# A spectral filter and a squared-ReLU feed-forward layer on one core: PSUM in three phases, index tables on GpSimd, constants folded into tables, the drain in another order

## The chip, the core and the metric

The kernel runs on one core of a Trainium2 chip. A core has five engines, each with its own instruction queue: TensorE (PE in the profile) multiplies matrices into PSUM, VectorE (DVE), ScalarE (ACT) and GpSimd (POOL) do element-wise work, and SyncE (SP) issues the transfers here. PSUM has eight banks of 512 float32 columns[...]. The metric is device time in microseconds from the start to the end of one execution. The span in the profile is the part of it between the first and the last instruction.

## The reference

The input x is 2048 rows by 512 columns in bfloat16. Two residual branches follow each other:

```python
h  = x + A(layernorm(x))          # A: irfft2(rfft2(x) * (w_r + 1j*w_i)) over both axes
h2 = h + B(layernorm(h))          # B: relu(h @ w1 + b1)**2 @ w2 + b2, 512 -> 1792 -> 512
```

A is a two-dimensional real Fourier transform over all 2048 rows and 512 columns, a product with a complex filter of 2048 by 257, and the inverse. So each row of the result of A depends on every row of x, and B can start only when A has ended for some rows.

## The kernel before

The 2048 rows are 16 tiles (g = 0 to 15) of 128 rows. The transforms are written as matrix products with sine tables that the kernel computes: GpSimd makes integer index tables (idxE, idxG, idxD), an index product such as `fiG` or `fiE` is formed by a multiplication with the partition number, and ScalarE turns it into bfloat16 with `Sin`. KF, EF, EI, GF and GI are the tables. EI and KI are transposes of EF and KF, made by a transfer (L432).

The first stage takes the mean and variance of each row tile (VectorE with bn_stats, L392, or ScalarE with two accumulating passes, L383 and L386, for tiles 5, 7, 9 and 11). In five batches of tiles, VectorE adds epsilon (L397), GpSimd raises to the power -0.5 (L399, `rs1`), and VectorE scales KF by it (L403, `KR`). TensorE multiplies x with KR (L415, L417, tiles p1 of PSUM), and ScalarE or VectorE copy the result into `Bt` (L423). Every tile of Bt is needed before the next step.

The middle stage works on eight pairs of blocks, pr = 0 to 7. For each: TensorE multiplies Bt with GF (p2, L485), a copy gives U (L494), TensorE multiplies with EF (p3, L511 to L550), ScalarE copies to AB (L517, L557), VectorE forms X (L564, only where the sum is not done by TensorE), then the products with the filter W, mA and mB (L574), their combination Z (L582) and the fold M (L593, L595). TensorE multiplies M with EI (p4, L609 to L615) and a copy gives T2 (L624).

The drain takes tiles 0 and 1 ahead of the others: d5 multiplies T2 with GI (L651), the copies are EO (L657), yt multiplies these back with a transposed output and is copied to UT0 (L664, L670), the first operand of the up-projection. The same rows in the straight order (py, L771 to L776) give the squares (L633, L786), the standard deviation `sd0` and, through a small matmul `sr` (L801), a row `srow` that scales the bias (L863).

The feed-forward stage goes over five chunks of rows, (0,2), (2,5), (5,9), (9,13), (13,16): up-projection (L859, 14 blocks), ReLU on ScalarE (L872), square on VectorE (L878), down-projection (L887), output (L896, L898). Between its matmuls TensorE also finishes A for the later tiles (p5 at L709 to L712, p6 at L732 or L739), which VectorE and ScalarE evacuate.

The order of instructions on each engine is decided while the program is built, by the class `Plan`. A task has an engine (or a choice of two), a cost, a priority, what it reads and writes, and perhaps a buffer of a pool with a set number of buffers. `run` repeatedly takes the task that can start first by these costs; tasks within SLACK of each other go by priority. `pin` then keeps this order in the program. Costs of transfers are issue times on SP and a lag to landing:

```python
add("SP", 1.2, lambda i=i: sy.dma_start(W[i][:, 0:9, :], wv[i][:, 0:9, 1:L + 1]), writes=[("Wn", i)],
    prio=20 + i, at=1.0, lag=7.0)
add("SP", 0.8, lambda i=i: sy.dma_start(W[i][:, 9:16, :], wx[i][:]), reads=[("wx", i)], writes=[("Wr", i)],
    prio=22 + i, lag=5.0)
```

The filter arrives in two parts of 9 and 7 block rows (`Wn`, `Wr`), each for the real and the imaginary half. The tables are scaled by WSC = 2/(2048*512) through GI (L454), where the last partition gets half of it through `hsc`. All PSUM tiles up to the drain come from one pool of four two-bank tiles (`mm_tile`); the feed-forward stage has one-bank tiles: three `ph`, two `po`, three `pp`. `warm` puts small matmuls on zeros in front of a tile where the planner sees TensorE idle.

Of the kernel before, what the change touches and what calls it, by code (L numbers as in the profile page):

```python
# [33 lines left out]
class Plan:  # L34
# [3 lines left out]
    SLACK = 0.15  # L38
# [51 lines left out]
    def run(self):  # L90
# [7 lines left out]
        while any(left.values()):  # L98
            best = None
            for e, ts in left.items():  # L100
                pick = None
                for t in ts:
# [13 lines left out]
                    if pick is None or r < pick[0] - self.SLACK:  # L116
                        pick = (r, t)
                    if r <= self.free[e] + 1e-9:
                        break
                if pick and (best is None or pick[0] < best[0] or (pick[0] == best[0] and e == "DVE")):  # L120
                    best = (*pick, e)
# [25 lines left out]
def kernel(  # L147
# [70 lines left out]
    hsc = fwd.tile([P, 1], FP32, name="hsc")  # L218
# [19 lines left out]
    ps = tc.alloc_tile_pool(name="ps", bufs=4, space=bass.MemoryType.PSUM)  # L238
# [4 lines left out]
    plan = Plan({"mm": 4, "U": 3, "AB": 3, "X": 2, "mA": 2, "mB": 2, "Z": 2, "M": 2, "st": 4, "EO": 2,  # L243
                 "ph": 3, "po": 2, "pp": 3, "rl": 6, "act": 2, "od": 2, "q": 2, "R": 3, "u2": 2, "qb": 2, "UT": 2, "ot": 3})
# [6 lines left out]
    def mm_tile(key, dt=FP32):  # L251
        T[key] = ps.tile([P, 4096 // mybir.dt.size(dt)], dt, tag="mm", name="m_" + str(key[0]))
        warm(T[key])
        return T[key]
# [8 lines left out]
    def lo(fi):  # L263
        return fi.bitcast(I16)[:, ::2]
# [35 lines left out]
    def iota(dst, pattern, base, cm):  # L300
# [17 lines left out]
    pool(0.1, lambda: gp.memset(mhalf[:], -0.5), 1.1, writes=["mhalf"])  # L318
# [4 lines left out]
    pool(0.1, lambda: gp.memset(hsc[:], WSC), 1.5, writes=["hsc0"])  # L323
    pool(0.2, lambda: gp.affine_select(out=hsc[:], in_=hsc[:], compare_op=ALU.not_equal, fill=0.5 * WSC, base=-(P - 1),
                                       pattern=[[0, 1]], channel_multiplier=1), 1.6, reads=["hsc0"], writes=["hsc"])

    pool(0.1, lambda: gp.memset(mv1[:], 0.0), 1.7, writes=["mv1z"])
# [13 lines left out]
    for t in range(2):  # L341
        for r in range(2):
            dve(0.36, lambda t=t, r=r: ve.tensor_scalar(fiG[:, t, r, :], idxG[:], pF[:, 3 + t:4 + t],
                                                        float((QT, HT)[r]), ALU.mult, ALU.add),
                0.6, reads=["pF", "idxG"], writes=[("fiG", t)], shared=True)
# [5 lines left out]
    act(1.28, lambda: sc.activation(fiE[0][:], idxE[:], ACT.Identity, scale=cE[:]), 0.3, reads=["idxE", "cE"],  # L351
        writes=["fiE0"])
# [12 lines left out]
    def fill(key, n, prio, reads=(), at=0.0):  # L365
        def go():
            p = mm_tile(key)
            for _ in range(n):
                mm(p[:, 0:512], lhsT=fz[:, 0:P], rhs=fz[:], start=True, stop=True)
        add("PE", n * 0.216, go, reads=["fz", *reads], writes=[key], prio=prio, alloc=("mm", key), at=at)  # L370
# [4 lines left out]
    ON_ACT = (5, 7, 9, 11)  # L375
    SQ = 6
    BATCH = ((0, 4), (4, 8), (8, 12), (12, 14), (14, 16))
    RT = float(1.0 / np.sqrt(D))
    for bi, (a, b) in enumerate(BATCH):
# [22 lines left out]
        for g in range(a, b):  # L402
            dve(0.22, lambda g=g: ve.tensor_scalar(flat(KR[:, g]), flat(KF[:]), rs1[:, g:g + 1], None, ALU.mult), z - 5,  # L403
                reads=[("rs", bi), "KF"], writes=[("KR", g)], shared=True)
    for j in range(8):
        key = ("p1", j)
        for i in range(2):
            g = 2 * j + i

            def s1(g=g, i=i, key=key):  # L410
                pt = mm_tile(key) if i == 0 else T[key]
                pv = pt[:].rearrange("p (t e i c) -> p t e i c", t=2, e=2, i=2)
                for t in range(2):
                    o = pv[:, t, :, i, :]
                    mm(o, lhsT=xs[:, g, P * t:P * t + P], rhs=KR[:, g, 0].unsqueeze(1).to_broadcast([P, 2, P]),  # L415
                       start=True, stop=False)
                    mm(o, lhsT=xs[:, g, 256 + P * t:256 + P * t + P], rhs=KR[:, g], start=False, stop=True)  # L417
            add("PE", 0.46, s1, reads=[("KR", g), ("x", g)], order=[("p1a", j)] * i,
                writes=[key, ("p1a", j) if i == 0 else ("p1b", j)], prio=10 + 2 * j, alloc=("mm", key) if i == 0 else None)

        def e1(j=j, lo_=0, hi=2, eng=sc.copy):
            dst = Bt[:].rearrange("p e q (g s) -> p e g q s", s=8)[:, :, 2 * j + lo_:2 * j + hi]
            eng(dst, T["p1", j][:].rearrange("p (e i q s) -> p e i q s", e=4, i=2, q=16)[:, :, lo_:hi])  # L423
        if j < 5:
            act(0.93, e1, 10 + 2 * j, reads=[key], writes=["Bt"])
        else:
            for i in range(2):
                add(("ACT", "DVE"), (0.59, 0.67), lambda e, j=j, i=i, e1=e1: e1(j, i, i + 1, COPY[e]),
                    reads=[("p1a" if i == 0 else "p1b", j)], writes=["Bt"], uses=[key], prio=56 + 2 * j)
# [17 lines left out]
    for lt in range(4):  # L447
        pool(0.48, lambda lt=lt: gp.tensor_scalar(fiI[:, lt], idxD[:], pF[:, 5 + lt % 2:6 + lt % 2],
                                                  float((QT, HT)[lt // 2]), ALU.mult, ALU.add), 2.0,
             reads=["pF2", "idxD"], writes=["fiI"])  # L450
    act(1.07, lambda: sin_of(flat(GI[:]), lo(flat(fiI[:]))), 27.0, reads=["fiI", ("KR", 13)], writes=["GI0"])
# [482 lines left out]
```

## Time and profile before

| | us |
|---|---|
| median of 3 runs | 178.74 (178.45 to 178.90) |
| the profiled execution | 178.47 |
| its span | 176.7 |
| TensorE busy | 164.3 (93%) |
| VectorE busy | 125.7 (71%) |
| ScalarE busy | 112.0 (63%) |
| GpSimd busy | 11.8 (7%) |
| up-projection L859, 280 matmuls | 54.8 busy |
| down-projection L887, 224 matmuls | 51.8 busy |

The ends of matmuls are modelled and overlap, so TensorE's busy share is not its share of peak; starts are measured. The profile lists groups of instructions by line and shape, the chain of work that ended last, DMA issues with the time to landing, and timelines by engine, in which a row has its start, its length and, in brackets, the idle time before it with what ended it. Times in it count from the start of the span. The mean granted TensorE clock is 0.998 of full speed.

### The profile page before, as it was taken

What the parts mean: (1) busy time and instruction counts of PE and PEld (TensorE: products, weight loads), DVE (VectorE), ACT (ScalarE), POOL (GpSimd) and SP (SyncE); (2) the same over time, 40 slices, a digit from 0 to 9 for tenths busy, and PEclk for the clock granted to TensorE, in tenths of its full rate; (3) what the DMA queues carried; (4) which work ended last, traced back from release to release, by engine and by line L of the source; (5) the groups of instructions that cost most, each with busy time, mean ns of one, the idle gap of its engine ahead of it and who ended that gap; (6) DMA issues with size and microseconds to landing.
All of it is one profiled execution on the core that took longest, in us unless ns stands there. A gap on an engine that the chain in (4) does not pass through costs nothing.

```text
span 176.7 us, 3029 instructions
## 1 busy us (share of the span) xinstructions
PE 164.3 (93%) x1123; PEld 96.5 (55%) x1123; DVE 125.7 (71%) x358; ACT 112.0 (63%) x203; POOL 11.8 (7%) x32
## 2 busy tenths in 40 slices
PE   7989669999987799998999999999999999999991
PEld 4478546776664565556655454444554445455540
DVE  4999558989984497356998569989369896156331
ACT  8799729998673646657889268665358663066400
POOL 8844100000000000000000000000000000000000
PEclk9999999999999999999999999999999999999999
DMA  5959999970000000000000100001100000100010
GB/s 139 338 138 164 257 302 298 383 228 0 4 0 0 0 4 0 0 32 33 0 0 0 61 32 0 0 2 58 36 30 0 0 0 33 59 30 0 4 59 30
DMA packets 15600, 12.16 MB, mean 69 GB/s; under 512 B 6112, under 2 KB 14176, under 8 KB 15586
## 3 DMA queue, kind: packets, MB, share of 16 engines
q1 hardware_dynamic: 15586, 11.97, 23.9%
q8 instruction: 9, 0.15, 0.4%
q14 instruction: 5, 0.04, 0.1%
HBM read 8.92 MB, written 3.01 MB: 68 GB/s over the span
## 4 chain that ended last, share of the span: by engine, by line
PE 69%; DVE 12%; ACT 10%; issue 3%; DMA 3%; SPq 0%; DVEq 0%; ACTq 0%
PE ph L859 28%; PE po L887 28%; ACT Bt L423 3%; DMA xs<-in_A_x_dram 3%; DVE Z L582 2%; PE pp L837 2%; DVE mA L574 2%; DVE mB L574 2%; ACT junk L383 2%; PE m_p L485 2%; ACT junk L386 2%; PE pp L739 1%; PE ph L863 1%; DVE M L593 1%; ACT AB L557 1%
## 5 line engine op out<-in xcount | busy, mean ns | idle before, releaser
L859 PE MATMUL ph<-UT,W 128*128 128x384 bf16 (+2 forms) x280 | 54.8, 337 | 0.7 <-ACT UT L845 0.7
L887 PE MATMUL po<-W,act 128*128 128x512 bf16 x224 | 51.8, 379 | 0.0
L872 ACT ACTIVATE rl<-ph,b1f 128x384 bf16<-128x384 f32 (+1 forms) x56 | 34.9, 632 | 24.8 <-PE ph L859 22.5
L859 PEld LDWEIGHTS <-W 128*128 128x128 bf16 x280 | 26.0, 98 | 20.9 <-issue 0.8
L878 DVE TENSOR_TENSOR act<-rl 128x384 bf16<-128x384 bf16 (+2 forms) x70 | 25.4, 368 | 14.3 <-ACT rl L872 13.3
L887 PEld LDWEIGHTS <-act 128*128 128x128 bf16 x224 | 21.5, 98 | 24.3 <-issue 0.4
L898 DVE TENSOR_TENSOR ot<-po,hb 128x512 bf16<-128x512 f32 x14 | 9.7, 692 | 17.1 <-PE po L887 16.9
L633 ACT ACTIVATE junk<-hs,nm 128x512 bf16<-128x512 bf16 x14 | 10.0, 714 | 1.9 <-DVE hs L760 1.8
L494 ACT CAST U<-m_p 128x1024 bf16<-128x1024 f32 (+1 forms) x8 | 9.2, 1194 | 2.7 <-DVE mhl L462 2.6
L763 DVE TENSOR_TENSOR hb<-hs,b2b 128x512 f32<-128x512 bf16 x16 | 10.7, 684 | 0.0
L760 DVE TENSOR_TENSOR hs<-pp,xs 128x512 bf16<-128x512 f32 x14 | 9.5, 685 | 0.3 <-PE pp L732 0.2
L624 ACT CAST T<-m_p 128x1024 bf16<-128x1024 f32 (+2 forms) x9 | 8.1, 904 | 2.5 <-PE m_p L615 1.8
L415 PE MATMUL m_p<-KR,xs 128*128 128x256 bf16 x32 | 7.2, 272 | 2.3 <-DVE KR L403 2.3
L824 ACT ACTIVATE u<-hs,nr,rs 128x512 bf16<-128x512 bf16 x8 | 6.2, 806 | 4.6 <-DVE nr L816 4.6
L485 PE MATMUL m_p<-GF,Bt 128*128 128x256 bf16 x64 | 8.0, 273 | 0.8 <-DVE Bt L423 0.8
L872 ACT ACTIVATE rl<-ph 128x256 bf16<-128x256 f32 x14 | 5.1, 383 | 5.7 <-PE ph L863 5.7
L557 ACT CAST AB<-m_p 128x1024 bf16<-128x1024 f32 x7 | 7.3, 1041 | 2.2 <-PE m_p L545 2.2
L249 PEld LDWEIGHTS <-fz 128*128 128x128 bf16 x115 | 7.6, 103 | 1.9 <-DVE pI L333 1.2
L615 PE MATMUL m_p<-EI,M 128*128 128x256 bf16 x56 | 7.9, 274 | 0.7 <-DVE M L593 0.5
L755 DVE TENSOR_TENSOR R<-q 128x127 bf16<-128x127 f32 x36 | 8.4, 285 | 0.0
L392 DVE BATCH_NORM_STATS2 st<-xs 128x6 f32<-128x512 bf16 x12 | 7.9, 663 | 0.0
L417 PE MATMUL m_p<-KR,xs 128*128 128x256 bf16 x32 | 7.2, 273 | 0.0
(191 smaller groups left out, 238.1 us busy)
## 6 DMA issues: line engine op xcount, KB each, us to landing
W<-in_B_w_dram SPq DMA_DIRECT2D x2, 1792.0 KB, 10.9
out_dram<-ot SPq DMA_DIRECT2D x16, 128.0 KB, 1.8
xs<-in_A_x_dram SPq DMA_DIRECT2D x3, 512.0 KB, 5.6
W<-wx SPq DMA_DIRECT2D x2, 448.0 KB, 6.6
W<-in_A_w_r_dram SPq DMA_DIRECT2D x1, 576.0 KB, 5.2
W<-in_A_w_i_dram SPq DMA_DIRECT2D x1, 576.0 KB, 7.2
xs<-in_A_x_dram SPq DMA_DIRECT2D x2, 256.0 KB, 3.7
wx<-in_A_w_r_dram SPq DMA_DIRECT2D x1, 448.0 KB
```

The lines of the kernel that those rows point to most:

```text
L485: mm(puv[:, q, e, :], lhsT=Bt[:, 2 * t + 1 - e, 2 * pr + q, :], rhs=gfv[:, t, :, e, :], start=(t == 0), stop=(t == 1))
L494: eng(U[:].rearrange("p q (c e) -> p q e c", e=2)[:, a:b], puv[:, a:b])
L557: sc.copy(t[:].rearrange("p u r c -> p (u r c)"), T["p3", pr][:])
L633: sc.activation(junk[:], src, ACT.Square, bias=nm1[:, g:g + 1], accum_out=ss2[:, g:g + 1])
L755: ve.tensor_tensor(o, x, y, (ALU.add, ALU.subtract, ALU.subtract, ALU.add)[k])
L760: dve(0.66, lambda g=g: ve.tensor_tensor(hs[:, g, :], T["p6", g][:], xs[:, g, :], ALU.add), z, reads=[("p6", g)], writes=[("hs", g)])
L763: dve(0.62, lambda g=g: ve.tensor_tensor(hb[:, g, :], hs[:, g, :], b2b[:], ALU.add), late + 180 + g, reads=[("hs", g), ("FW", 3), ("ph", c ...
L859: mm(p[:, 0:P * n], lhsT=W1[:, d, bass.ts(f, P)], rhs=(T["UT", c] if c else UT0)[:, d, 0:P * n], start=(d == 0), stop=(d == ND - 1 and c > 0))
L872: sc.activation(r[:, 0:P * n], T["ph", c, f][:, 0:P * n], ACT.Relu, bias=b1f[:, f:f + 1] if c else 0.0, scale=1.0)
L878: ve.tensor_tensor(t[:, f, 0:P * n], r[:, 0:P * n], r[:, 0:P * n], ALU.mult)
L887: mm(p[:], lhsT=T["act", c][:, f, bass.ts(i, P)], rhs=W2[:, f, :], start=(f == 0), stop=(f == NF - 1))
L898: ve.tensor_tensor(o[:], T["po", g][:], hb[:, g, :], ALU.add)
```

## The change

Six things change together.

- *The planner.* SLACK goes from 0.15 to 0.08, and a task is now picked by priority among all within SLACK of the earliest. The whole order is planned anew.
- *PSUM.* The program is planned in three phases. Phase a (the first stage) has two two-bank tiles (`mm`) and four one-bank tiles (`sg`); tiles 10 to 15 of p1 are one-bank tiles. Phase b has three two-bank tiles and two one-bank tiles; p2 of pairs 0 and 1, p3 of pair 0, mr and yt are one-bank tiles. Phase c has one `ph`, two `po`, three `pp` and the two `sg` that stay; up-projections rotate over ph, sg, sg. In the columns of p1 the two tiles of a two-bank tile now have a bank each.
- *Index tables.* The four `fiG` go from VectorE and `fiE[0]` from ScalarE to GpSimd. `fiI` is made after the last `rs1`, and the Sin for GI in the middle stage.
- *Constants.* WSC is a second multiplier of KR. `hsc` and the scaling of GI go; the half for the last partition is now a half for the last column of W (L-1), in place, by four GpSimd instructions, two for the first 9 rows and two for the last 7.
- *Statistics.* ScalarE takes tiles 3, 5, 7 and 9. The square-root table is loaded after p4 of pair 5 in place of 6.
- *Drain.* The last T2 is copied in halves by PSUM bank. d5 has a one-bank tile per product, from the pools of phase c. py comes ahead of the up-projection, UT0 of tile 0 is for VectorE and of tile 1 for ScalarE. Some waits in the feed-forward stage become orders.

```diff
-    SLACK = 0.15
+    SLACK = 0.08
...
-                    if pick is None or r < pick[0] - self.SLACK:
-                        pick = (r, t)
+                    cand.append((r, t))
                     if r <= self.free[e] + 1e-9:
                         break
+                pick = None
+                if cand:
+                    first = min(r for r, _ in cand) + self.SLACK
+                    pick = next(c for c in cand if c[0] <= first)
...
-    plan = Plan({"mm": 4, "U": 3, "AB": 3, "X": 2, "mA": 2, "mB": 2, "Z": 2, "M": 2, "st": 4, "EO": 2,
-                 "ph": 3, "po": 2, "pp": 3, "rl": 6, "act": 2, "od": 2, "q": 2, "R": 3, "u2": 2, "qb": 2, "UT": 2, "ot": 3})
+    plan = Plan({"mm": 2, "sg": 4, "U": 3, "AB": 3, "X": 2, "mA": 2, "mB": 2, "Z": 2, "M": 2, "st": 4, "EO": 2,
+                 "ph": 1, "po": 2, "pp": 3, "rl": 6, "act": 2, "od": 2, "q": 2, "R": 3, "u2": 2, "qb": 2, "UT": 2, "ot": 3})
...
-    pool(0.1, lambda: gp.memset(hsc[:], WSC), 1.5, writes=["hsc0"])
-    pool(0.2, lambda: gp.affine_select(out=hsc[:], in_=hsc[:], compare_op=ALU.not_equal, fill=0.5 * WSC, base=-(P - 1),
-                                       pattern=[[0, 1]], channel_multiplier=1), 1.6, reads=["hsc0"], writes=["hsc"])
...
-            dve(0.36, lambda t=t, r=r: ve.tensor_scalar(fiG[:, t, r, :], idxG[:], pF[:, 3 + t:4 + t],
-                                                        float((QT, HT)[r]), ALU.mult, ALU.add),
-                0.6, reads=["pF", "idxG"], writes=[("fiG", t)], shared=True)
+            pool(0.46, lambda t=t, r=r: gp.tensor_scalar(fiG[:, t, r, :], idxG[:], pF[:, 3 + t:4 + t],
+                                                         float((QT, HT)[r]), ALU.mult, ALU.add),
+                 1.95, reads=["pF", "idxG"], writes=[("fiG", t)])
...
-    act(1.28, lambda: sc.activation(fiE[0][:], idxE[:], ACT.Identity, scale=cE[:]), 0.3, reads=["idxE", "cE"],
-        writes=["fiE0"])
+    pool(1.4, lambda: gp.tensor_scalar(fiE[0][:], idxE[:], cE[:], 0.0, ALU.mult, ALU.add), 0.95, reads=["idxE", "cE"],
+         writes=["fiE0"])
...
-            dve(0.22, lambda g=g: ve.tensor_scalar(flat(KR[:, g]), flat(KF[:]), rs1[:, g:g + 1], None, ALU.mult), z - 5,
+            dve(0.22, lambda g=g: ve.tensor_scalar(flat(KR[:, g]), flat(KF[:]), rs1[:, g:g + 1], WSC, ALU.mult, ALU.mult), z - 5,
...
-                                                  float((QT, HT)[lt // 2]), ALU.mult, ALU.add), 2.0,
-             reads=["pF2", "idxD"], writes=["fiI"])
-    act(1.07, lambda: sin_of(flat(GI[:]), lo(flat(fiI[:]))), 27.0, reads=["fiI", ("KR", 13)], writes=["GI0"])
...
-    for e in range(2):
-        dve(0.35, lambda e=e: ve.tensor_scalar(GI[:, e::2], GI[:, e::2], hsc[:] if e else WSC, None, ALU.mult), 180.0,
-            reads=["GI0", "hsc"], writes=["GI"], shared=True)
+                                                  float((QT, HT)[lt // 2]), ALU.mult, ALU.add), 400.0,
+             reads=["pF2", "idxD", ("rs", 4)], writes=["fiI"])
...
+        act(1.07, lambda: sin_of(flat(GI[:]), lo(flat(fiI[:]))), 125.0, reads=["fiI"], writes=["GI"])
...
+    for k, (a, b) in (("n", (0, 9)), ("r", (9, 16))):
+        for i in range(2):
+            pool(0.15, lambda i=i, a=a, b=b: gp.tensor_scalar(W[i][:, a:b, L - 1:L], W[i][:, a:b, L - 1:L], 0.5, None,
+                                                              ALU.mult), 300.0,
+                 reads=[("W" + k, i)], writes=[("Wh" + k, i)])
...
+            plan.run()
+            ps.release()
+            psg = ctx.enter_context(tc.tile_pool(name="psg", bufs=2, space=bass.MemoryType.PSUM))
+            ps = tc.alloc_tile_pool(name="psb", bufs=3, space=bass.MemoryType.PSUM)
...
-            act(0.32, lambda: et(7, 0, 2), z, reads=[("p4", 7)], writes=["T2a"])
...
+            for h in range(2):
+                add(("ACT", "DVE"), (0.25, 0.22), lambda e, h=h, et=et: et(COPY[e], 7, h, 2, 0, 2), prio=z, reads=[("p4", 7)],
+                    writes=["T2a", ("T2a", h)])
+                add(("ACT", "DVE"), (0.53, 0.6), lambda e, h=h, et=et: et(COPY[e], 7, h, 2, 2, 16), prio=z + 90,
+                    reads=[("p4", 7)], order=["T2a"], writes=["T2", ("T2r", h)])
...
-        add(("ACT", "DVE"), (0.58, 0.67), ute, reads=[("yt", g, 2)], writes=[("UT", 0)], uses=[("yt",)], prio=z + g)
+        add((("DVE", "ACT")[g],), (0.67 - 0.09 * g,), ute, reads=[("yt", g, 2)], writes=[("UT", 0)], uses=[("yt", g)],
+            prio=z + g)
```

## The prediction, made before the changed kernel ran

> **What bounds the kernel now.** I read the page's chain first. It says that the feed-forward matmuls own more than half of the span, and the change does not touch how many there are.
>
> ```profile
> PE 69%; DVE 12%; ACT 10%; issue 3%; DMA 3%; SPq 0%; DVEq 0%; ACTq 0%
> ```
>
> The busy time by stretches has TensorE at 19.78 of 20 us between 80 and 100, and at 20.00 of 20 from 100 to 160. What can move lies before about 80 us, so I went through the chain in order of time there.
>
> ```profile
> 49.80 0.60 DVE mA L574
> 50.40 0.61 DVE mB L574
> 51.04 0.77 DVE Z L582 x2
> 51.90 0.42 DVE M L593
> 52.32 0.35 DVE M L595
> 52.72 0.94 PE m_p L615 x7
> ```
>
> This pattern fills 37.4 to 52.7: VectorE is the bound of the middle stage, at 2.87 us a pair of blocks. I use four marks: the first column transform (L485) starts at 23.02, the last M ends at 52.67, the first up-projection (L859) starts at 59.74, the first bias matmul (L863) at 62.36. Ahead of 23.02 the timelines of VectorE, GpSimd and the DMA queue matter.
>
> ```profile
> 19.05 1.29 DVE L423 CAST Bt<-m_p 128x512 bf16<-128x512 f32 x2 [1.32 <-ACT Bt L423]
> 20.26 0.47 DVE L403 TENSOR_SCALAR KR<-KF,rs 128x256 bf16<-128x256 bf16 x2
> ```
> ```profile
> 16.23 0.70 POOL L399 TENSOR_TENSOR rs<-rs,mhalf 128x2 f32<-128x2 f32 x1 [1.53 <-DVE rs L397]
> 17.82 0.70 POOL L399 TENSOR_TENSOR rs<-rs,mhalf 128x2 f32<-128x2 f32 x1 [0.89 <-DVE rs L397]
> ```
> ```profile
> 9.68 4.57 SPq L432 DMA_TRANSPOSE EI<-EF  x1
> 14.35 1.18 SPq L432 DMA_TRANSPOSE KI<-KF  x1
> 15.58 0.58 SPq L286 DMA_DIRECT2D W<-in_A_w_r_dram  x1
> 16.22 1.59 SPq L286 DMA_DIRECT2D W<-in_A_w_i_dram  x1
> 17.91 1.63 SPq L288 DMA_DIRECT2D W<-wx  x2
> ```
> ```profile
> W<-wx SPq DMA_DIRECT2D x2, 448.0 KB, 6.6
> W<-in_A_w_r_dram SPq DMA_DIRECT2D x1, 576.0 KB, 5.2
> W<-in_A_w_i_dram SPq DMA_DIRECT2D x1, 576.0 KB, 7.2
> ```
>
> The fence just above is the list of DMAs, last column from issue to landing. Together: the reciprocal roots rs of the last two batches are made at 16.2 and 17.8, while the filter W lands at 15.58+5.2 = 20.8, 16.22+7.2 = 23.4, 17.91+6.6 = 24.5 and about 19.2+6.6 = 25.8. Today nobody reads W before 27.63 (first mA), so its lateness is free. The VectorE fence shows a loss of another kind: its half of a two-bank tile waits for ScalarE's half, and KR stands behind it.
>
> [...] KR above waits out the 1.32 us of the Bt ahead of it. [...] with the last matmul starting before 173.1, the clock (third column from the right) is below 1.00 between 175 and 176.7.
>
> ```profile
> 173.00:174.00 1.00, 0.06 (x1) 0.00 (x0) 0.69 (x1) 0.00 (x0) 0.00 (x0) 1.00 0.00 0
> 174.00:175.00 1.00, 0.00 (x0) 0.00 (x0) 0.00 (x0) 0.00 (x0) 0.00 (x0) 1.00 0.31 114
> 175.00:176.70 1.70, 0.00 (x0) 0.00 (x0) 0.00 (x0) 0.00 (x0) 0.00 (x0) 0.79 0.03 10
> ```
>
> **The change part by part.** The positions come from the built program's order of instructions and waits, the durations from this trace.
>
> *Tables and constants.* VectorE loses four fiG (1.41 us) and two GI scalings (0.28+0.34); ScalarE loses fiE0 (1.26); GpSimd loses hsc (0.23+0.19) and the zeroing of mv, and gains fiE0 (1.41, as fiE1) and fiG (4 at 0.46, as fiI). GpSimd now works until 3.4+1.41+1.05+1.41+1.84 = 9.1, so rs of batch 0 ends near 10.2 and KR starts near 10.55 (10.24 today): +0.3. EF0 starts at 4.86 in place of 3.46, and ScalarE with eight statistics passes (6.4), two GF and EF1 reaches its first Bt at 14.5 (13.89 today): +0.6. Folding WSC into KR adds a second constant to an existing instruction: nothing.
>
> *Halving the edge column of W.* Four small GpSimd instructions, perhaps 0.15 to 0.3 us each (GpSimd's smallest rows take 0.10 to 0.23; none has this form). Their own time is nothing; their place is everything. The order on GpSimd is: rs of batches 0, 1, 2; edge of W real and imaginary (9 rows); rs of batch 3 (tiles 12, 13); edges of the other 7 rows; rs of batch 4 (tiles 14, 15); fiI. Each edge waits for its DMA. So rs 3 waits for 23.4: 23.45+0.15+0.70 = 24.35. On VectorE, KR 12, 13 is queued behind that, and with it the sum for batch 4, Bt of tile 11, CN and KR 14, 15. rs 4 waits for 25.8: 25.8+0.15+0.70 = 26.65, KR 14 at 26.72. Today KR 14 starts at 20.26 and the column transform 2.76 later; one-bank tiles let both engines evacuate at once, which takes 0.7 of it. New start: 26.72+2.06 = 28.8, against 23.02: **+5.8 us**. SP's order is unchanged, so the landings should be too.
>
> *Clock.* With tile 11 done near 20.3, TensorE would wait 4.4 us for tile 12. If the clock falls, tiles 12 to 15 and the first column transforms run at half rate: eight steps of 0.43 on the path at the worst, less what hides, 0 to 2 us. I take 0.8.
>
> *Middle stage.* Up to the first mA I find 4.6 us after the column transform starts, as today (27.63-23.02): the split tiles save waits, and two one-bank buffers make TensorE wait for evacuations. Then the new ScalarE order is AB0, GI, AB1, U2, mrow, U3, T0, U4, AB2. With 1.05, 0.95, 1.2, 0.3, 1.2, 0.95, 1.15 and 0.95 after AB0 at 4.6, AB2 is ready at 12.35. VectorE has finished Z0 at 6.7, and X1 to M1 at 10.4, and idles 2.0 us where today it idled 0.31 once (X at 37.39). GI, moved here (1.10), is half of this. Bounds: 0 if casts overlap better, 2.5. Net **+1.4**.
>
> *Drain.* Today from the last M to the first up-projection 7.07. After: p4 ends +1.03; then VectorE 0.25, ScalarE 0.25, VectorE 0.6, ScalarE 0.55 evacuate one after the other, because the tile still has two banks; the waits show each for the other, and the first d5 waits for the last of them: 2.9. d5 to 3.76, EO to 4.35, py0 and yt0 to 4.85, py1 and yt1 to 5.93, then UT0 of tile 1 on ScalarE to 6.73: **-0.3** only. But py, the squares and sd now run in front of the up-projection, so the bias row is ready at 8.65, against 9.69 today, and the next projections at about 10.5 against 12.0. Together **-1.4**. At the turn to the second chunk (75 to 80) TensorE idles 0.45 today; nine down-projection matmuls now cover the last transpose: **-0.4**. Otherwise the feed-forward matmuls and their three-deep tiles are the same: 0, within 0.5.
>
> Sum: 5.8+0.8+1.4-1.4-0.4 = +6.2. The profiled execution took 178.47 us (span 176.7), 0.27 below the median of the runs, so 184.7 on its scale and about 184.8 us as a median.
>
> **Rivals.**
> (1) *The stall comes, and is soaked up.* The clock stays up, casts overlap and the drain pays 1 us more: 178.7+5.8-2.5 = about 182. For it: in the middle ScalarE had 2.2 us of waits. Against: ScalarE's order is fixed.
> (2) *The stall, then a cold clock in full.* Clock 2, ScalarE's queue 2.5: about 187. For it: the fall of the clock shown above.
> (3) *No stall, not slower.* The place is rs 3 and rs 4 on GpSimd. If W were there when rs 3 could run (about 17) and rs 4 (about 20.7), KR 14 would start at 21.6, the column transform at 23.65: +0.6+1.4-1.8 = +0.2, 179.0 us, no difference that can be told. It decides from a landing before about 20; each us later than that is a us lost. For it: the planner's costs assume landings near 17 to 18 (1.0 us for a transpose that took 4.57 to issue). Against: four landings in the trace.
> (4) *The one-bank tiles are worth more than I see*, removing also the 1.3 us waits of VectorE before AB and T, with no stall: 0.6-1.3-1.0 = -1.7, about 177. Nothing in the profile lifts the waits on W.
>
> **How the numbers follow.** My forecast, with its own range 183 to 186.5: 0.66. Rival 1: 0.12; rival 2: 0.12; rival 3: 0.06; rival 4: 0.04. The range for 8 in 10 is 181.6 to 187.2: it takes in the bounds of the clock and of ScalarE's queue, and leaves out rivals 3 and 4 and part of the ends. No change is within 0.3%, about what a measurement of this kernel can tell: faster 0.05, same 0.05, slower 0.90.
>
> **What would show it.** In the changed kernel GpSimd's rs of batch 3 starts after 23.4 and that of batch 4 after 25.7, with DMA waits ahead; VectorE shows an idle stretch of some 4 us before KR 12; the first column transform starts at 28.8 or later; VectorE idles about 2 us before the second X; the last M ends near 60; the granted clock is below 1.00 around 22 to 30 if the third term is right. It is wrong if W lands before 20, or if the column transform starts before 25.

## The result: slower by 5.4 us

The changed kernel takes 184.25 us (median of 4, 183.55 to 184.53); the kernel before took 178.82 beside it. The ratio is 1.030, with a 95% interval of 1.027 to 1.033. The forecast was 184.8 with a range of 181.6 to 187.2. The profiled execution took 184.32 us, its span is 182.5, against 178.47 and 176.7 before: +5.8 in the span.

One thing is needed to read the numbers below: in some executions of most versions, the one before included, the granted TensorE clock falls to half (0.50 in the profiles, for 3.41 or 6.83 us) and the time is 1.3 to 3.3 us longer, so smaller differences are drawn between executions with a mean clock of 0.996 or more, called "clock up".

My four marks and the end of the span in the two profiles (starts, but for the last M, which is its end), with the change from one mark to the next in the last column:

| | before | after | |
|---|---|---|---|
| first column transform | 23.02 | 31.23 | +8.2 |
| last M ends | 52.67 | 60.82 | -0.1 on the way |
| first up-projection | 59.74 | 67.47 | -0.4 |
| first bias matmul | 62.36 | 69.41 | -0.7 |
| end of the span | 176.7 | 182.5 | -1.2 |

All the loss, and more, is there when the column transform starts. From then on the changed kernel gains 2.4 us.

In what follows, KR 14 is KR of tile 14, and rs 3 and rs 4 are the reciprocal roots of the last two batches, for tiles 12, 13 and 14, 15. The edge of W is the last column, which the change halves on GpSimd.

### The profile page after: what moved, and what is told of

Its sections match the earlier page's. It is cut to its first block, busy times and chain, and to the rows that moved or that the text cites. A ratio compares the mean times of both kernels' runs of the same rounds, so it can differ in the third digit from the quotient of the medians.

```text
span 182.5 us, 2994 instructions
## 1 busy us (share of the span) xinstructions
PE 164.4 (90%) x1096; PEld 97.7 (54%) x1112; DVE 123.6 (68%) x350; ACT 110.3 (60%) x206; POOL 15.3 (8%) x38
## 4 chain that ended last, share of the span: by engine, by line
PE 75%; DVE 9%; DMA 7%; SPq 2%; issue 2%; ACT 2%; POOL 1%; POOLq 0%; DVEq 0%; ACTq 0%
PE po L913 26%; PE sg L885 18%; PE ph L885 9%; DMA xs<-in_A_x_dram 4%; DMA W<-wx 4%; PE m_p L513 3%; DVE st L398 2%; PE pp L862 2%; DVE KR L409 2%; PE m_p L643 1%; SPq L295 1%; PE pp L764 1%; DVE Z L610 1%; PE pp L757 1%; PE s_p L513 1%
## 5 line engine op out<-in xcount | busy, mean ns | idle before, releaser
L913 PE MATMUL po<-W,act 128*128 128x512 bf16 x215 | 49.9, 379 | 0.4
L885 PE MATMUL sg<-UT,W 128*128 128x512 bf16 (+2 forms) x182 | 37.7, 337 | 0.1
L885 PEld LDWEIGHTS <-W 128*128 128x128 bf16 x280 | 25.9, 98 | 20.6 <-issue 0.3
L898 ACT ACTIVATE rl<-sg,b1f 128x512 bf16<-128x512 f32 (+1 forms) x37 | 23.2, 634 | 18.8 <-PE sg L885 17.4
L904 DVE TENSOR_TENSOR act<-rl 128x384 bf16<-128x384 bf16 (+2 forms) x70 | 24.9, 367 | 9.6 <-ACT rl L898 9.1
L885 PE MATMUL ph<-UT,W 128*128 128x384 bf16 (+2 forms) x96 | 20.4, 335 | 0.3 <-ACT UT L717 0.2
L898 ACT ACTIVATE rl<-ph,b1f 128x384 bf16<-128x384 f32 (+1 forms) x19 | 12.0, 630 | 4.3 <-PE ph L885 3.6
L420 PE MATMUL s_p<-KR,xs 128*128 128x256 bf16 x12 | 4.3, 364 | 6.1 <-DVE KR L409 6.0
L409 DVE TENSOR_SCALAR KR<-KF,rs 128x256 bf16<-128x256 bf16 x16 | 4.0, 307 | 7.2 <-POOL rs L405 7.2
L849 ACT ACTIVATE u<-hs,nr,rs 128x512 bf16<-128x512 bf16 x7 | 5.6, 810 | 3.7 <-DVE nr L841 3.7
L422 PEld LDWEIGHTS <-xs 128*128 128x128 bf16 x32 | 3.5, 108 | 7.9 <-issue 7.3
```

The costliest lines, as they stand in the source:

```text
L885: mm(p[:, 0:P * n], lhsT=W1[:, d, bass.ts(f, P)], rhs=(T["UT", c] if c else UT0)[:, d, 0:P * n], start=(d == 0), stop=(d == ND - 1 and c > 0))
L898: sc.activation(r[:, 0:P * n], T["ph", c, f][:, 0:P * n], ACT.Relu, bias=b1f[:, f:f + 1] if c else 0.0, scale=1.0)
L904: ve.tensor_tensor(t[:, f, 0:P * n], r[:, 0:P * n], r[:, 0:P * n], ALU.mult)
L913: mm(p[:], lhsT=T["act", c][:, f, bass.ts(i, P)], rhs=W2[:, f, :], start=(f == 0), stop=(f == NF - 1))
```

## The profile after

The shares of the chain of work that ended last, and the granted clock over 40 slices of the span, from the page:

```profile
PE 75%; DVE 9%; DMA 7%; SPq 2%; issue 2%; ACT 2%; POOL 1%; POOLq 0%; DVEq 0%; ACTq 0%
```
```profile
PEclk9999966999999999999999999999999999999999
```

DMA has gone from 3% of the chain to 7%, and GpSimd, which had no share, is in it. The clock is down in slices 6 and 7, from 22.8 to 32. GpSimd's timeline shows where (start, length, instruction, and in brackets the idle time before it and what ended it):

```profile
22.10 0.29 POOL L488 TENSOR_SCALAR W<-W 128x9 bf16<-128x9 bf16 x1 [6.89 <-DMA W<-in_A_w_r_dram]
24.81 0.28 POOL L488 TENSOR_SCALAR W<-W 128x9 bf16<-128x9 bf16 x1 [2.42 <-DMA W<-in_A_w_i_dram]
25.02 0.73 POOL L405 TENSOR_TENSOR rs<-rs,mhalf 128x2 f32<-128x2 f32 x1
25.95 0.38 POOL L488 TENSOR_SCALAR W<-W 128x7 bf16<-128x7 bf16 x1 [0.20 <-DMA W<-wx]
27.13 0.27 POOL L488 TENSOR_SCALAR W<-W 128x7 bf16<-128x7 bf16 x1 [0.80 <-DMA W<-wx]
27.34 0.73 POOL L405 TENSOR_TENSOR rs<-rs,mhalf 128x2 f32<-128x2 f32 x1
28.07 1.86 POOL L453 TENSOR_SCALAR fiI<-idxD,pF 128x256 int32<-128x256 int32 x4
```

The rs of the last two batches stand behind the edge of W: 25.02 and 27.34, where the kernel before had 16.23 and 17.82. VectorE passes it on:

```profile
18.84 0.69 DVE L430 CAST Bt<-s_p 128x512 bf16<-128x512 f32 x1 [2.18 <-PE s_p L422]
25.78 0.48 DVE L409 TENSOR_SCALAR KR<-KF,rs 128x256 bf16<-128x256 bf16 x2 [6.25 <-POOL rs L405]
...
28.11 0.98 DVE L409 TENSOR_SCALAR KR<-KF,rs 128x256 bf16<-128x256 bf16 x2 [0.97 <-POOL rs L405]
```

Before, KR 14 and 15 stood behind a Bt that waited 1.32 us for ScalarE's half; now KR 12 and 13 wait 6.25 us for GpSimd, and KR 14 and 15 another 0.97. The chain in order of time joins the pieces:

```profile
19.13 6.74 DMA W<-wx
25.95 0.38 POOL W L488
...
27.40 0.68 POOL rs L405
28.11 0.54 DVE KR L409
...
31.23 1.92 PE s_p L513 x16
```

The program waits for a filter that nobody multiplies with before 34.67. The busy time by stretches (PE, its weight loads, DVE, ACT, POOL; third from the right the granted clock) shows what TensorE makes of it:

```profile
22.00:24.00 2.00, 0.00 (x0) 0.00 (x0) 0.00 (x0) 0.00 (x0) 0.29 (x1) 0.94 1.11 316
24.00:26.00 2.00, 0.00 (x0) 0.00 (x0) 0.22 (x2) 0.00 (x0) 0.99 (x3) 0.50 1.05 376
26.00:28.00 2.00, 1.88 (x11) 1.39 (x11) 1.13 (x5) 0.59 (x1) 1.20 (x3) 0.50 1.29 190
```
```profile
26.12 0.37 PE L420 MATMUL s_p<-KR,xs 128*128 128x256 bf16 x1 [6.01 <-DVE KR L409]
```

It is idle for 6.0 us, and then does tiles 12 to 15 at half clock (0.50 from 23.76 to 30.59).

The landings themselves were later than before: W's four parts at about 22.0, 24.7, 25.9 and 27.1, against 20.8, 23.4, 24.5 and 25.8. SP issued them later, behind a transpose that began later (10.51 against 9.68), since the two copies into wx ahead of it held SP's queue until 10.4 and not 9.6:

```profile
10.51 4.78 SPq L437 DMA_TRANSPOSE EI<-EF  x1
...
16.63 0.58 SPq L295 DMA_DIRECT2D W<-in_A_w_r_dram  x1
```

In the middle stage, VectorE has its first mA 3.44 us after the column transform (4.61 before). Its copy of one half of AB no longer waits for ScalarE's copy of the other: the first line is of the kernel before, the other two are of VectorE and ScalarE in the changed kernel.

```profile
26.90 0.69 DVE L517 CAST AB<-m_p 128x512 bf16<-128x512 f32 x1 [1.38 <-ACT AB L517]
```
```profile
33.62 0.69 DVE L544 CAST AB<-s_p 128x512 bf16<-128x512 f32 x1
```
```profile
34.05 0.59 ACT L544 CAST AB<-s_p 128x512 bf16<-128x512 f32 x1
```

Later VectorE waits for ScalarE's AB twice:

```profile
34.67 0.69 DVE L602 TENSOR_TENSOR mA<-AB,W 128x1024 bf16<-128x1024 bf16 x1 [0.36 <-ACT AB L544]
...
37.28 0.76 DVE L589 TENSOR_TENSOR X<-AB 128x512 bf16<-128x512 bf16 x2 [0.52 <-ACT AB L582]
...
42.80 0.76 DVE L589 TENSOR_TENSOR X<-AB 128x512 bf16<-128x512 bf16 x2 [1.85 <-ACT AB L582]
```

## The experiments

The theory: GpSimd's place for the edge of W is the whole loss, and the rest of the change gains. The rivals: the rest is worth nothing or loses; the lateness has another source; the cold clock is the larger part.

### The edge of W behind the last rs

```diff
-                 reads=[("W" + k, i)], writes=[("Wh" + k, i)])
+                 reads=[("W" + k, i), ("rs", 4)], writes=[("Wh" + k, i)])
```

> The changed kernel with one edit: the four edge halvings of W stand behind the last rs on GpSimd. Theory (the stall is the loss, and the rest of the change gains): KR 14 starts near 21, the first column transform near 24 in place of 31.2, TensorE has no idle stretch of 6 us before tile 12 and its granted clock stays at 1.0 there; the median falls from 184.3 by 6 to 7.5, to 177 to 178.3, which is below the kernel before (178.8). GI's index table now comes after the last edge (27.1+0.3), near 29.3, and may hold ScalarE up by about 1 us. Rival (the rest of the change is worth nothing): 178.8 to 179.5, as my rival 3 had it. Rival (the lateness comes from elsewhere, such as the later landings or the index tables): 180 or more, the column transform at 26 or later.

Measured: 180.11 us, ratio to before 1.003 (1.000 to 1.005), 178.62 to 183.15 over 20 executions, none with a mean clock above 0.990. The stall is gone: KR 14 at 22.28, the column transform at 24.32. The time isn't what I expected, and the rival "worth nothing" would fit it by chance. The timelines of GpSimd, ScalarE and VectorE say why not:

```profile
27.47 3.23 POOL L453 TENSOR_SCALAR fiI<-idxD,pF 128x256 int32<-128x256 int32 x4
```
```profile
30.73 1.06 ACT L270 ACTIVATE GI<-fiI 128x1024 bf16<-128x1024 int16 x1 [3.00 <-POOL fiI L453]
```
```profile
32.72 0.76 DVE L589 TENSOR_TENSOR X<-AB 128x512 bf16<-128x512 bf16 x2 [2.74 <-ACT AB L582]
```

I had put 1 us to GI's table coming last; it cost ScalarE 3.00 and VectorE 2.74, of which 1.4 are the table's own time (3.23 us beside a busy VectorE and not 1.86). TensorE, too, had lost its clock from 15.43 to 18.84, ahead of any of this (more below). Why the clock fell in all 20 executions of this version is not shown by one profile.

### GI's table first, then the edge

```diff
-             reads=["pF2", "idxD", ("rs", 4)], writes=["fiI"])
+             reads=["pF2", "idxD", ("KR", 15)], writes=["fiI"])
...
-                 reads=[("W" + k, i)], writes=[("Wh" + k, i)])
+                 reads=[("W" + k, i), "fiI"], writes=[("Wh" + k, i)])
```

> As the run before, but GI's index table (four GpSimd products) is made straight after KR 15 and the edge halvings of W come after it. Theory: the column transform near 24, no wait of ScalarE for GI's table, 176.7 to 177.7; and KR 14 and 15, which took 0.98 us for two in the changed kernel while GpSimd made that table, take 0.48 again. Rival (the 0.98 us are not from GpSimd): KR 14 and 15 still 0.9 or more.

Measured: 176.97 us, ratio 0.988 (0.982 to 0.994); 176.03 twice with the clock up, 177.90 and 179.12 where it fell. GpSimd's timeline:

```profile
19.88 0.70 POOL L405 TENSOR_TENSOR rs<-rs,mhalf 128x2 f32<-128x2 f32 x1 [2.28 <-DVE rs L403]
20.57 1.95 POOL L453 TENSOR_SCALAR fiI<-idxD,pF 128x256 int32<-128x256 int32 x4
22.48 0.29 POOL L488 TENSOR_SCALAR W<-W 128x9 bf16<-128x9 bf16 x1
23.67 0.28 POOL L488 TENSOR_SCALAR W<-W 128x9 bf16<-128x9 bf16 x1 [0.89 <-DMA W<-in_A_w_i_dram]
```

The same instructions still wait for W to land, but nothing is queued behind them. The column transform starts at 22.92. Against the changed kernel that is 8.31 us earlier, and the profiled executions differ by 8.29 (184.32 - 176.03): the place of four instructions of 0.3 us is the whole loss, with what follows from it (the cold clock, and KR beside the table). Against the kernel before, this version gains 2.4 us with the clock up (176.03 to 178.47). So the rest of the change gains. My expectation, 176.7 to 177.7, holds for the median; with the clock up it was 0.7 too high.

The part on KR was not tested by this run: the dependence on KR 15 only orders the plan, and the table began at 20.57, with KR 14 and 15 at 20.64 and 0.70 long for the two. The run before answers it. There GpSimd did nothing while KR 14 and 15 ran, and they took 0.48; in the changed kernel, beside the table, 0.98.

### The edge alone, in the kernel before

```diff
-                 ... flat(KF[:]), rs1[:, g:g + 1], None, ALU.mult)
+                 ... flat(KF[:]), rs1[:, g:g + 1], WSC, ALU.mult, ALU.mult)
...
-         dve(0.35, lambda e=e: ve.tensor_scalar(GI[:, e::2], GI[:, e::2], hsc[:] if e else WSC, None, ALU.mult), 180.0,
-             reads=["GI0", "hsc"], writes=["GI"], shared=True)
+             pool(0.15, lambda i=i, a=a, b=b: gp.tensor_scalar(W[i][:, a:b, L - 1:L], W[i][:, a:b, L - 1:L], 0.5, None,
+                                                               ALU.mult), 300.0,
+                  reads=[("W" + k, i)], writes=[("Wh" + k, i)])
...
```

What is left out here takes hsc away and lets mA and mB read the halved W.

> The kernel before with one part of the change alone: WSC is a second multiplier of KR, GI is not scaled, and four GpSimd instructions halve the edge column of W. Here GpSimd's order is: W real 9 rows, W real 7 rows, rs 3, W imaginary 9 rows, rs 4, W imaginary 7 rows. Theory: rs 3 waits for the landing of the 7 real rows (24.5), ends at 25.6, KR 14 starts at 27.0 to 27.5 in place of 20.26, the column transform at 30 to 31, the median 178.8+7 = 185 to 187: this part alone loses what the whole change loses, and more than a us on top, since nothing of its gains is there. Rival (the loss comes from planning PSUM and the tables anew): within 1 us of 178.8.

Measured: 188.93 us, ratio 1.057 (1.053 to 1.062): this part alone loses 10, more than I expected. Column transform at 32.90, +9.9, and the same +9.8 at the last M, the first up-projection and the end of the span. VectorE:

```profile
26.63 0.48 DVE L398 TENSOR_SCALAR KR<-KF,rs 128x256 bf16<-128x256 bf16 x2 [8.87 <-POOL rs L394]
...
29.00 0.69 DVE L418 CAST Bt<-m_p 128x512 bf16<-128x512 f32 x1 [1.22 <-PE m_p L412]
29.61 0.47 DVE L398 TENSOR_SCALAR KR<-KF,rs 128x256 bf16<-128x256 bf16 x2
```

rs 4 ended at 28.0, 1 us later than I had it, and KR 14 then stood behind a Bt that waited for TensorE, whose clock was down from 24.23 to 31.06. I had left that clock out of the estimate. The rival, within 1 us of before, is ruled out.

### TensorE kept busy during the stall

```diff
+             if g == 12:
+                 for _ in range(27):
+                     mm(pt[:], lhsT=fz[:, 0:P], rhs=fz[:], start=True, stop=True)
```

> The changed kernel with 27 matmuls on zeros (5.75 us at full clock) in front of tile 12, in the PSUM tile of tile 12, so that TensorE is busy during the stall. Nothing waits for them longer than for rs 3. Theory: the stall stays (KR 12 near 25.8), the granted clock stays at 1.0 up to 30, the column transform starts at 30.3 in place of 31.2, the median falls by 0.7 to 1.2: that is the price of the cold clock. Rival (my 2 us bound): it falls by 1.8 or more. Rival (KR, not the clock, paces tiles 12 to 15): under 0.4.

Measured: 184.33 us over all executions, no different from the changed kernel, but 182.51 in the one with the clock up. In the profiled one (184.65) the clock holds through the stall and the column transform starts at 29.97, not 31.23. Of these 1.26 us, 0.47 are a landing that was earlier in this execution (KR 14 at 27.64, not 28.11); from KR 14 to the column transform it is 2.33 against 3.12. So the clock is worth 0.8 there. (The execution with the clock up is 1.7 under the median of the changed kernel; it has no trace, so what of that is an earlier landing stays open.) And why was the profiled execution no faster in the end? Its clock fell later, from 62.13 to 65.54, in the drain, within this wait of TensorE:

```profile
62.34 1.01 PE L702 MATMUL po<-GI,T 128*128 128x256 bf16 x4 [1.78 <-ACT T L656]
```

From the start of the last M to the first up-projection it took 8.64 us, where the changed kernel took 7.07: a fall there costs 1.6.

### W loaded ahead of the transposes

The edge halvings stay in the bad place; the filter comes earlier.

```diff
-             prio=20 + i, at=1.0, lag=7.0)
+             prio=10 + i / 10, at=1.0, lag=7.0)
...
-             prio=22 + i, lag=5.0)
+             prio=10.5 + i / 10, lag=5.0)
...
-         add("SP", 1.0, lambda: sy.dma_start(dst, src, transpose=True), reads=dep, writes=[("EI", i)], prio=prio, lag=6.0)
+         add("SP", 1.0, lambda: sy.dma_start(dst, src, transpose=True), reads=dep, writes=[("EI", i)], prio=prio, lag=6.0,
+             order=[("Wr", 0), ("Wr", 1)])
```

> The changed kernel with its edge halvings where they were, between the rs of the last batches, but on SP all four loads of W issue ahead of the table transposes. It puts my rival 3 to the test: the loss is a us for each us that W lands late. W's 9 rows should land near 16 to 17, its 7 rows near 21 to 23 (they need the copy wx, near 15). Theory: rs 4 ends 1 us after the last landing that stands ahead of it, and the column transform starts 2.2 to 2.8 us after that, at 25 to 26.5 in place of 31.2. The transposes then issue until about 31, so p4 of pair 0 and all behind it may wait for EI; if not, the median is 178.5 to 180, and if so up to 184. Rival (GpSimd's instructions themselves, not their waits, cost the time): the column transform stays after 29.

Measured: 181.24 us, ratio 1.012 (1.008 to 1.015). W landed later than I thought (edges at 18.64 to 23.84), and so the column transform is later than the 25 to 26.5 that I expected. But the time follows the landing:

```profile
23.84 0.33 POOL L489 TENSOR_SCALAR W<-W 128x7 bf16<-128x7 bf16 x1 [0.33 <-DMA W<-wx]
24.19 0.73 POOL L405 TENSOR_TENSOR rs<-rs,mhalf 128x2 f32<-128x2 f32 x1
```

rs 4 ends at 24.92, not 28.07: 3.15 earlier. The column transform starts at 28.18: 3.05 earlier. The median is 3.0 lower. In this run a us of landing is a us of time; the instructions are the same. The column transform came 3.26 after rs 4, where I had 2.2 to 2.8, because the clock was down here as well (24.43 to 27.84) and KR 14 and 15 ran beside GpSimd's table again (0.98). No wait for EI appeared between the column transform and the last M, 29.6 us as elsewhere.

### Fillers ahead of the wait, not behind it

From here on, the version with GI's table first is the base. Its TensorE waits before tile 4 for ScalarE's first Bt, since phase a has two two-bank tiles where the kernel before has four. The planner sees the gap and fills it with small matmuls on zeros (fillers), but in the tile that TensorE waits for:

```profile
14.92 1.50 PE L253 MATMUL m_p<-fz 128*128 128x128 bf16 x24 [1.52 <-ACT Bt L430]
16.26 0.27 PE L420 MATMUL m_p<-KR,xs 128*128 128x256 bf16 x1
```

They start when the wait is over, and hold tile 4 up by 1.34 us. The edit puts eight larger ones in another tile, ahead of the wait:

```diff
+     fill(("fb", 0), 8, 13.5, reads=[("KR", 3), ("p1", 1)])
```

> The run that makes GI's table after KR 15 and halves the edge of W last (176.03 us where the clock stayed up, 177.9 and 179.12 where it fell), with eight matmuls on zeros more, behind tile 3 and ahead of the wait for ScalarE's first Bt. Theory: TensorE's idle stretch of 1.5 to 2.2 us before tile 4 (two two-bank tiles, both waiting for ScalarE, where the kernel before has four) is what lets the granted clock fall near 15.4 in some executions, for 3.4 us. Filled, it falls in none there: median 176.0 to 176.5, spread under 1.2 us, mean clock 0.998 or more in nearly all. Rival (the clock falls elsewhere, in the drain): spread and median as before the edit, 177 or more.

Measured: 176.19 us, ratio 0.981 (0.976 to 0.985). With the clock up, 174.81 and 174.97: 1.1 under the base, which I had not expected, since the planner now leaves two of its 24 fillers:

```profile
12.79 1.89 PE L375 MATMUL s_fb<-fz 128*128 128x512 bf16 x8
15.10 0.27 PE L253 MATMUL m_p<-fz 128*128 128x128 bf16 x2 [0.43 <-ACT Bt L432]
```

The column transform starts at 21.87. But four of six executions still ran at 0.986 or 0.987 and 176.2 to 176.5. So the median is where I had it, but not for my reason, and the rival is right that the clock also falls elsewhere. The next two runs ask whether that is the drain.

```diff
+                 if (g, e) == (0, 1):
+                     for _ in range(8):
+                         mm(p[:], lhsT=fz[:, 0:P], rhs=fz[:], start=True, stop=True)
```

> As the run before, with eight matmuls on zeros more in the drain, in the bank of the first d5, ahead of its wait for the last T2. If the clock falls in the drain in some executions (it did at 62.1 in the run with fillers in the stall, where the drain from the last M to the first up-projection took 1.5 us longer), this run alone is steady at 176.0 to 176.4. If the drain is not where it falls, the two runs agree within 0.3 us, or this one is up to 0.3 slower, where the fillers delay d5.

Measured: 177.35 us, ratio 0.988 (0.983 to 0.994); 176.53 with the clock up, 1.6 worse than without these fillers. I had made the planner's mistake myself: these fillers, too, waited 1.78 us for ScalarE's last T2, and d5 stands behind them.

```profile
54.46 3.38 PE L702 MATMUL po<-fz 128*128 128x512 bf16 x8 [1.78 <-ACT T L655]
57.68 0.60 PE L704 MATMUL po<-GI,T 128*128 128x256 bf16 x4
```

This profile has a fall from 54.11 to 57.52, so the place was right. The mended form puts them into a free two-bank tile of the phase before, straight behind the last p4:

```diff
+     def fd():
+         p = mm_tile(("fd", 0))
+         for _ in range(8):
+             mm(p[:, 0:512], lhsT=fz[:, 0:P], rhs=fz[:], start=True, stop=True)
+     add("PE", 1.73, fd, reads=["fz"], order=[("p4", 7, 1)], writes=[("fd", 0)], prio=400.0, alloc=("mm", ("fd", 0)))
```

> The run with fillers behind tile 3 (174.9 us where the clock stayed up, 176.2 to 176.5 where its mean was 0.986), with eight matmuls on zeros more (1.7 us) behind the last p4, in a free two-bank tile, where TensorE waits 1.8 us for ScalarE's last copy of T2. The fillers wait for nothing that is late, and d5 is not to be delayed. Theory: the clock falls in the drain, and these fillers keep it up: 174.8 to 175.2 in nearly all executions, mean clock 0.998 or more. Rival (it falls elsewhere): half of the executions at 176.2 to 176.5 and 0.986 as before. Rival (the fillers delay d5, as the eight in d5's own bank did): 175.4 or more with a clock of 1.0.

Measured: 174.91 us (174.88 to 175.41 in five, all with a mean clock of 0.999 or 1.0), ratio to before 0.978 (0.975 to 0.981).

```profile
52.62 1.89 PE L671 MATMUL m_fd<-fz 128*128 128x512 bf16 x7
54.66 0.60 PE L706 MATMUL po<-GI,T 128*128 128x256 bf16 x4
```

d5 comes 3.15 us after p4 of the last pair starts; without the fillers 3.06 (54.24 - 51.18). They cost nothing that shows. In the five other runs with fillers behind tile 3 but not in this place, the clock was down in 21 of 38 executions; here in none of five. This version beats both kernels: 9.3 us under the changed one, 3.8 under the one before.

### Parts of the gain undone

All three are edits of the run with fillers behind tile 3 (174.81 and 174.97 with the clock up). First py, back behind both yt:

```diff
-                        prio=-5000.5 + g, alloc=(("pp", "po")[g], ("py", g)) if k == 0 else None)
+                        prio=early - 9 + g, alloc=(("pp", "po")[g], ("py", g)) if k == 0 else None)
```

> The first run of this set with one thing undone: py, the rows in straight order, comes behind both yt on TensorE as in the kernel before, not ahead of each. Theory: the first up-projection starts 0.3 to 0.6 us earlier, the squares, sd and the bias row 0.3 to 0.6 later, and since the fourth projection waits for the bias row through its PSUM tile, the median rises by 0.2 to 0.7: this order is about a third of the drain's gain of 1.3. Rival (the order is worth nothing, the gain is in the split copies and banks): within 0.15 us of the first run.

Measured: 175.19 to 175.22 with the clock up, +0.3. From the last M's start the first up-projection comes 0.28 earlier (6.80 against 7.08), the first bias matmul 0.86 later (9.87 against 9.01). So the order is worth about 0.3. The first projection came earlier and the end later, so it is the bias row that decides, not the first projection. The other 2 us that the change gains behind the last M were not taken apart.

Next p2 of pairs 0 and 1 back in two-bank tiles, and then p3 of pair 0 as well:

```diff
-                pu = sg_tile(("p2", pr, q)) if pr < 2 else mm_tile(("p2", pr)) if q == 0 else T["p2", pr]
+                pu = mm_tile(("p2", pr)) if q == 0 else T["p2", pr]
...
-                o = sg_tile(("p3", 0, u))
+                o = (mm_tile(("p3", 0)) if u == 0 else T["p3", 0])[:, 512 * u:512 * u + 512]
```

> The run with fillers behind tile 3, with one part of the change undone: p2 of pairs 0 and 1 is one two-bank tile for both halves, as in the kernel before, where the change has a one-bank tile for each half. The order of instructions on each engine stays. In the changed kernel the first mA stands 3.44 us after the column transform, before 4.61, which I had not foreseen. Theory (two engines evacuate the halves of p2 at once only where they have a tile each): that distance goes from 3.50 back to 4.3 to 4.8 us, and the median rises by 0.8 to 1.3. Rival (it comes from p3 of pair 0 or from GI having left ScalarE's queue there): 3.4 to 3.7 us, and no more than 0.2.

> The run with p2 of pairs 0 and 1 in two-bank tiles (first mA 3.99 us after the column transform, 175.3 us with the clock up), with p3 of pair 0 in one two-bank tile as well, as in the kernel before. Theory (the other half of what I missed): VectorE's half of AB waits for ScalarE's half, the first mA goes to 4.4 to 4.7 us after the column transform, and the median with the clock up to 175.7 to 176.1. Rival (the rest comes from elsewhere): 4.0 to 4.1 us, 175.3.

Measured with p2 alone: first mA 3.99 us after the column transform, not 3.50, and 175.29 to 175.56 with the clock up, +0.4: half of what I expected. With p3 too: 5.09 us and 176.38 to 176.49, +1.5, more than I expected. (The clock of this profile fell at 26.74, too late to bear on the 5.09 us.) VectorE and then ScalarE in that last run:

```profile
25.38 0.69 DVE L546 CAST AB<-m_p 128x512 bf16<-128x512 f32 x1 [1.01 <-PE m_p L542]
26.78 0.69 DVE L604 TENSOR_TENSOR mA<-AB,W 128x1024 bf16<-128x1024 bf16 x1 [0.71 <-POOL W L490]
```
```profile
26.11 0.59 ACT L546 CAST AB<-m_p 128x512 bf16<-128x512 f32 x1 [0.97 <-DVE AB L546]
```

The halves of AB go one after the other (25.38, then 26.11), as they did in the kernel before, and mA starts when ScalarE's is done (26.70). The profile names GpSimd's W for mA's wait, but W does not decide: in the run without these two edits mA started at 25.37, ahead of the last two edges of W (25.58 and 26.90). So the one-bank tiles are what takes the 1.1 to 1.2 us out between the column transform and the first mA.

The 5.09 us are more than p3 alone, since they are above the 4.61 of the kernel before. TensorE's first p3 starts 2.63 us after the column transform in this run and 1.87 with p2 alone. It stands behind ScalarE's copy of U, which frees p2's tile: the program plans p2 of pairs 0 and 1 and p3 of pair 0 together with the first stage, in phase a and not in phase b as the list of changes has it, and that phase has two two-bank tiles, where the kernel before has four. The kernel before is the cleaner comparison for p3. Its two p3 start 1.87 and 2.63 us after the column transform, as they do in the run with p2 alone, and its mA comes at 4.61 against 3.99. So p2's tiles are worth 0.5 us (3.50 to 3.99) and p3's 0.6 (3.99 to 4.61).

## Why the prediction was right, by its own steps

**The mechanism** was right in each link: GpSimd's rs behind the edge of W, KR behind it on VectorE, the column transform behind that. Undoing it takes back 8.29 us of the profiled time, and in the one run that moved the landings the time moved with them, 3.0 us for 3.15.

**Column transform, +5.8.** Measured +8.2 together with the clock, for which I had 0.8. The step that failed is "SP's order is unchanged, so the landings should be too". W's last part landed at 27.06, not 25.8, so KR 14 stood at 28.11, not 26.72: +1.4. It isn't a fixed amount: with the same order on SP, the edge of the 9 imaginary rows began at 24.81 in the changed kernel, and at 24.98, 23.67 and 24.26 in three of its variants. From KR 14 to the column transform I had 2.06. With GpSimd quiet and the clock up (the run with the edge behind rs) it is 2.04. The changed kernel took 3.12: 0.3 from KR beside GpSimd's table, which I had not thought of (2.33 with fillers, against 2.04), and 0.8 from the clock.

**Clock, +0.8.** It measures 0.8 there. The half rate in it was my assumption ahead of the run, since the profile before shows no more than a mean of 0.79 over its last 1.7 us; in the stall of the changed kernel the clock is at 0.50. But I had it for one place only. The gaps before tile 4 and in the drain are places of their own, and a fall in the drain cost 1.6.

**Middle stage, +1.4.** Measured -0.1: an error of 1.5, and the other large one. "Up to the first mA I find 4.6 us, as today" is the step that failed: it is 3.44. The one-bank tiles of p2 and p3 let both engines evacuate at once, and I took that gain only for Bt in the first stage, and wrote it off here against waits of TensorE that didn't come. ScalarE's queue was nearly right: from the first mA to the last M it is 26.15 against 25.04, +1.1, with VectorE idle 0.52 and 1.85 ahead of two X; I had AB2 as the late one, and it is.

**Drain, -1.4, and the turn to the second chunk, -0.4.** First up-projection -0.4 (I said -0.3), bias row -1.1 (-1.0). TensorE's wait of 0.67 us at the turn (up to 80.22 before) is gone. All from the last M to the end: -2.3, against -1.8. d5 waits 1.78 us for ScalarE's last T2, as I had it.

**The sum** came out at +6.2, against +5.8 in the span and +5.4 in the medians. This is in part luck: my column transform, clock included, was 1.6 short (6.6, measured 8.2), my middle stage 1.5 too long and my drain 0.5 too small a gain. The last step of the sum is also 0.1 off: 178.74 + 6.2 is 184.9, not 184.8.

**The rivals.** The third, no stall and 179.0, was right on where it decides and wrong on what is left then: without the stall it is 176.0 with the clock up, 3 us below, closer to my fourth (177). The first stage has nothing to show for the +0.6 that I gave it (22.92 against 23.02), the middle stage not the +1.4, and the drain is 0.5 better. By that rival's sum I would have called "no change" for a version that is 1.4% faster.

## What to carry to other kernels

Before an instruction that waits for a DMA is put on an engine, look at what that engine has queued behind it: here four instructions of 0.3 us, which wait for late landings, cost 8.3 us ahead of two small instructions, and held up nothing that shows behind them and the table. A filler that keeps TensorE's clock up belongs in a PSUM tile that is free when the gap begins; in the tile that TensorE waits for it starts after the gap and only delays (here by 1.34 us before tile 4, and by 1.6 us of the whole time in the drain; in a free tile all five executions had a mean clock of 0.999 or more). And when a sum of parts comes out right, the parts still want checking one by one.

## What the runs showed of the hardware

- The granted clock fell to 0.50 for 3.41 us (six falls) or 6.83 us (two, in the stalls of the changed kernel and of the edge alone), in all profiles where it fell inside the work. TensorE need not have been idle for as long as that before a fall: in the first run above it fell at 15.43, when TensorE had been idle from 12.7 to 14.9, that is 2.2 us, and in the drain it fell three times at a wait of 1.78 us (at 62.13, 54.11 and 57.46). The traces say more when each is divided into stretches of 3.41 us, counted back from a change of its clock. Three of them, with TensorE's busy time first: the one ahead of the fall at 15.43, then two of the changed kernel that no fall followed.

```profile
12.02:15.43 3.41, 1.22 (x17) 1.00 (x15) 3.41 (x14) 3.41 (x6) 1.64 (x2) 1.00 1.00 170
```
```profile
13.52:16.94 3.42, 1.82 (x29) 1.77 (x29) 3.15 (x15) 2.46 (x4) 1.15 (x1) 1.00 1.09 169
61.31:64.72 3.41, 1.57 (x14) 1.21 (x13) 1.49 (x4) 1.18 (x4) 0.00 (x0) 1.00 0.00 0
```

  In the stretches ahead of the eight falls TensorE was idle for 1.96 to 3.41 us. No stretch inside the work with 1.84 us idle or less was followed by a fall, and none with more escaped one. So in these profiles the line lies near 1.9 of 3.41 us: an estimate from these eight falls, with the ends of matmuls modelled. By it, where a gap is cut decides whether a fall follows. The changed kernel's own wait of 2.02 us before tile 4 (13.10 to 15.12) was cut at 13.52 into stretches with 1.17 and 1.60 idle, and the clock stayed up; the gap of 2.2 us in the first run lay within one stretch, and it fell. This is a reading of the profiles; no run tested it by itself.
- VectorE's KR, two in 0.48 us, took 0.98 beside GpSimd's index product (0.70 in the run where both began together); and four of these products took 3.23 us beside VectorE's middle stage, not 1.86. What makes the two engines hold each other up is not shown. The change moved work to GpSimd, which is busy for 15.3 us (8%); by these numbers that work was not free beside a busy VectorE: 0.50 us of VectorE's time for two KR, and 1.4 us more for GpSimd's table.
